# A GEGLU FFN on one core: two staged sums interleaved row by row in DRAM, and one operand sum cut in halves with GpSimd's next sums ordered behind it

## Chip, cores, metric

One core of a Trainium2 chip. The metric is the device time of one execution in microseconds, lower is better. The kernel before: 540.52 us, median of 3 runs (540.35 to 541.16).

## Reference

```python
def reference(x, w_gate, w_up, w_down):          # x (1, 2048, 1024), F = 3584, all bf16
    return (_gelu(x @ w_gate) * (x @ w_up)) @ w_down
```

## The kernel before

Both halves of the FFN are computed with seven products for eight (a Strassen-Winograd scheme): M1 to M7 from sums S1 to S4 of the left blocks and T1 to T4 of the right blocks. In the gate/up part a "pair" of feature blocks is one such scheme for gate and one for up (j = 0, 1): 14 accumulations of 4 matmuls. VectorE makes the T sums of the activations, GpSimd the S sums of the weights one pair ahead. In the down projection, T sums are sums of rows of `w_down`; T2 and T4 are computed during the gate/up part of the first half, staged in DRAM, and loaded back two rows at a time.

```python
t_dram = dram_pool.tile([P, 2, NS, DN], F32, name="t_dram")     # NS = 14 rows, DN = 512

def stage_step(n):                   # gate/up part, first half: rows of T2 (k=1), T4 (k=2)
    ...
    if k > 0:
        sp(nc.sync.dma_start(out=t_dram[:, k - 1, i, :], in_=t.bitcast(F32)))

def t_down(grp, name, i0, i1):       # down projection, two rows at a time
    ...
            if name in ("t2", "t4"):
                src = t_dram[:, 0 if name == "t2" else 1, i : i + 2, :]
                sp(nc.sync.dma_start(out=t.bitcast(F32), in_=src))
```

In the down projection a ring of 20 rows holds the T sums of one product and part of the next one, so the last loads of T2 can only be issued as TensorE frees rows of T1: four loads of 512 KB in a burst, 0.9 us apart (four issued in 3.06 us from 234.17 in the trace of the kernel before). There are eight such bursts (T2 and T4, two token groups, two halves).

The pair code, with the part that concerns pair 1 of the first half (the only pair of the first weight chunk that goes through it, and the only one that runs M2 at once):

```python
def do_m5(j):
    mm(V_[j], j, s(j, "s1"), tsum["t1"], True)
    m5[j] = m_pool.tile([P, TB], F32, name=f"m5_{j}")
    act(nc.scalar.copy(out=m5[j][:], in_=banks[V_[j]][:]))
    prep(j, "s1")                                  # GpSimd: S1 of the next pair

def do_m6(j):
    mm(QB[j], j, s(j, "s2"), tsum["t2"], False)
    act(nc.scalar.copy(out=banks[RB[j]][:], in_=banks[QB[j]][:]))
...
elif "m2" in then:
    m2(); done("m2")                               # hooks: A22 copies, then T4 on VectorE
    order = (do_m5, 0), (do_m5, 1), (do_m6, 0), (do_m6, 1)
...
for j in range(2):
    add_m5(QB[j], QB[j])                           # VectorE, before M3
    prep(j, "s2")
done("m5")
for j in range(2):
    mm(RB[j], j, s(j, "s3"), tsum["t3"], False)    # M7
    add_m5(V_[j], RB[j])                           # VectorE; releases R for M4
    ...
# then M3 (into Q, with S4), then M4 (into R, with T4)
```

## Time and profile before

| | before |
|---|---|
| time, median (lowest to highest) | 540.52 us (540.35 to 541.16) |
| span of the profiled run | 538.7 us |
| TensorE / VectorE / ScalarE / GpSimd busy | 99 / 67 / 49 / 45% |
| an undisturbed pair | 12.56 us |
| landing of the 56 staged loads, median | 5.3 us |

The lines behind the engines and the pair stand in the prediction; the landing is this line of the page:

```profile
t_mem<-t_dram SPq DMA_DIRECT2D x56, 512.0 KB, 5.3
```

"Landing" is the time from issue to the arrival of the last byte. The chain of work that ended last lists pieces in order of time: start, duration, what ran; a piece that is not TensorE's is a place where TensorE waited.

### The profile page before, as it was taken

Reading aid. Unit: us, or ns where it says so; the run is one execution under the profiler, and the core shown is the slowest. Engines: PE = TensorE matmul, PEld = TensorE weight load, DVE = VectorE, ACT = ScalarE, POOL = GpSimd, SP = SyncE. Lnnn points to the kernel's source line nnn. Section 1 sums busy time; section 2 is a strip of 40 time slices with the busy share of each in tenths; the row PEclk is TensorE's granted clock in tenths of the full one; section 3 lists DMA queues with packets and bytes.
Section 4 is the critical chain, followed back from the end, with each engine's and each line's share of the span. In section 5 each row is a group of like instructions: output and inputs, shape, how many; then the busy total and the mean of one; then the engine's idle time right before and its main releaser. Section 6 shows DMA issues by size and latency. Waiting matters only on the chain.

```text
span 538.7 us, 7074 instructions
## 1 busy us (share of the span) xinstructions
PE 532.4 (99%) x2348; PEld 377.6 (70%) x2384; DVE 362.1 (67%) x474; ACT 263.3 (49%) x446; POOL 244.6 (45%) x212
## 2 busy tenths in 40 slices
PE   9999999999999999999999999999999999999997
PEld 4577776677776686776776777777777766866865
DVE  2978767788775997989574334444454469969951
ACT  2555555555555329117465555555555551552270
POOL 0699777777776000000056776667777730000000
PEclk9999999999999999999999999999999999999999
DMA  9946776685818877779950404042222466677945
GB/s 217 324 118 194 213 244 204 229 258 190 292 60 263 302 235 252 246 262 300 326 177 1 156 1 158 22 135 71 86 78 80 157 211 215 229 240 238 293 147 204
DMA packets 84803, 102.70 MB, mean 191 GB/s; under 512 B 18720, under 2 KB 66336, under 8 KB 84768
## 3 DMA queue, kind: packets, MB, share of 16 engines
q1 hardware_dynamic: 61968, 80.30, 46.2%
q10 hardware_dynamic: 22800, 21.96, 13.1%
q8 instruction: 19, 0.31, 0.2%
q14 instruction: 16, 0.13, 0.1%
HBM read 85.98 MB, written 12.58 MB: 183 GB/s over the span
## 4 chain that ended last, share of the span: by engine, by line
PE 97%; DMA 1%; issue 0%; ACT 0%; ACTq 0%
PE bank L396 63%; PE bank L672 31%; PE bank L249 3%; DMA t_mem<-t_dram 1%; PE bank L202 1%; PE bank L293 0%; ACT o_sb L725 0%; ACT bank L450 0%; ACTq L725 0%; ACTq L450 0%
## 5 line engine op out<-in xcount | busy, mean ns | idle before, releaser
L396 PE MATMUL bank<-t_mem,s_mem 128*128 128x512 f32 x1056 | 249.4, 394 | 0.0
L396 PEld LDWEIGHTS bank<-t_mem,s_mem 128*128 128x128 f32 x1056 | 198.2, 188 | 43.8 <-ACT bank L446 0.3
L368 POOL TENSOR_TENSOR s_mem<-w_mem 128x512 fp32r<-128x512 bf16 x102 | 120.0, 1198 | 190.7 <-DVE t_mem L244 103.3
L672 PE MATMUL bank<-t_mem,s_mem 128*128 128x512 f32 x544 | 127.4, 393 | 0.1
L273 DVE TENSOR_TENSOR hT<-w_mem,bank 128x512 bf16<-128x512 f32 x104 | 71.3, 686 | 81.4 <-PE bank L396 46.3
L672 PEld LDWEIGHTS bank<-t_mem,s_mem 128*128 128x128 f32 x544 | 102.1, 188 | 22.6 <-DVE t_mem L580 0.5
L419 DVE TENSOR_TENSOR bank<-bank,m 128x512 f32<-128x512 f32 x108 | 69.9, 695 | 45.8 <-ACT m L441 44.0
L396 PE MATMUL bank<-xT,w_mem 128*128 128x512 bf16 x405 | 96.5, 380 | 1.4
L268 ACT ACTIVATE w_mem<-bank 128x512 f32<-128x512 f32 x104 | 61.9, 596 | 51.8 <-DVE bank L419 34.1
L396 PEld LDWEIGHTS <-w_mem 128*128 128x128 bf16 x432 | 40.2, 98 | 51.6 <-issue 6.8
L368 POOL TENSOR_TENSOR s_mem<-w_mem,s_mem 128x512 fp32r<-128x512 bf16 x52 | 66.5, 1304 | 0.0
L580 DVE TENSOR_TENSOR t_mem<-w_mem 128x1024 fp32r<-128x1024 bf16 x56 | 65.6, 1219 | 0.0
L368 POOL TENSOR_TENSOR s_mem<-s_mem,w_mem 128x512 fp32r<-128x512 f32 x52 | 60.7, 1189 | 0.0
L446 ACT COPY bank<-bank 128x512 f32<-128x512 f32 x54 | 30.8, 570 | 38.9 <-PE bank L396 38.9
L381 ACT CAST s_mem<-w_mem 128x512 fp32r<-128x512 bf16 x54 | 33.1, 615 | 31.6 <-PE bank L396 30.4
L647 DVE TENSOR_TENSOR s_mem<-hT 128x512 fp32r<-128x512 bf16 x52 | 34.2, 686 | 10.2 <-PE bank L672 9.4
L441 ACT COPY m<-bank 128x512 f32<-128x512 f32 x54 | 31.7, 587 | 17.5 <-PE bank L396 17.5
L672 PEld LDWEIGHTS <-hT 128*128 128x128 bf16 x224 | 21.3, 98 | 26.6 <-issue 2.1
L450 ACT COPY bank<-bank 128x512 f32<-128x512 f32 x54 | 30.7, 570 | 12.7 <-PE bank L396 12.5
L725 ACT CAST o_sb<-bank 128x512 bf16<-128x512 f32 x28 | 15.4, 585 | 39.6 <-PE bank L672 39.6
L605 DVE TENSOR_TENSOR o_sb<-wd_sb,o_sb 128x512 fp32r<-128x512 bf16 x28 | 30.5, 1090 | 0.5
L577 ACT CAST t_mem<-w_mem 128x1024 fp32r<-128x1024 bf16 x28 | 26.9, 1048 | 0.0
(42 smaller groups left out, 236.0 us busy)
## 6 DMA issues: line engine op xcount, KB each, us to landing
t_mem<-t_dram SPq DMA_DIRECT2D x56, 512.0 KB, 5.3
w_mem<-in_w_gate_dram ACTq DMA_DIRECT2D x10, 1024.0 KB, 5.2
w_mem<-in_w_up_dram ACTq DMA_DIRECT2D x10, 1024.0 KB, 5.5
wd_sb<-in_w_down_dram SPq DMA_DIRECT2D x28, 256.0 KB, 4.3
t_dram<-o_sb SPq DMA_DIRECT2D x28, 256.0 KB, 2.4
wd_sb<-in_w_down_dram SPq DMA_DIRECT2D x12, 512.0 KB, 8.4
w_mem<-in_w_down_dram SPq DMA_DIRECT2D x10, 512.0 KB, 6.1
w_mem<-in_w_down_dram SPq DMA_DIRECT2D x4, 1024.0 KB, 6.4
```

Of the source, the lines that this page charges most:

```text
L268: act(nc.scalar.activation(out=g_sb, in_=ps[:], func=ACT.Gelu_apprx_tanh))
L273: nc.vector.tensor_tensor(out=hT[:, fc, tb * TB : (tb + 1) * TB], in0=g_sb, in1=ps[:], op=ALU.mult,)
L368: pool(nc.gpsimd.tensor_tensor(out=t, in0=in0, in1=in1, op=op))
L381: act(nc.scalar.copy(out=t, in_=a(1, 1)))
L396: nc.tensor.matmul(banks[bank][:], lhsT=lhs[:, c, :], rhs=rhs[:, c, :], start=start and c == 0, stop=c == KH - 1, skip_group_check=True,)
L419: nc.vector.tensor_tensor(out=banks[dst][:], in0=banks[src][:], in1=m5[j][:], op=ALU.add)
L441: act(nc.scalar.copy(out=m5[j][:], in_=banks[V_[j]][:]))
L446: act(nc.scalar.copy(out=banks[RB[j]][:], in_=banks[QB[j]][:]))
L450: act(nc.scalar.copy(out=banks[QB[j]][:], in_=banks[P_[j]][:]))
L580: dve(nc.vector.tensor_tensor(out=t, in0=in0, in1=in1, op=ALU.subtract))
L647: dve(nc.vector.tensor_tensor(out=t, in0=in0, in1=in1, op=op))
L672: nc.tensor.matmul(banks[bset[u]][:], lhsT=lhs(i, u), rhs=rhs(i), start=start and i == 0, stop=stop and i == NS - 1, skip_group_check=True,)
```

## The change

Two parts. The intent of the first is faster loads of the staged rows (2 KB pieces, T2 and T4 of a row next to each other); that of the second is to keep a 2.7 us VectorE instruction out of the way of the adds behind it, and VectorE and GpSimd out of each other's way (side by side in pair 1 of the kernel before, T4 took 2.66 us and two S4 sums 4.36).

```diff
-    t_dram = dram_pool.tile([P, 2, NS, DN], F32, name="t_dram")
+    t_dram = dram_pool.tile([P, NS, 2, DN], F32, name="t_dram")
...
-            prep(j, "s1")                      # in do_m5; and the same for "s2"
+            if not eager:
+                prep(j, "s1")
...
+        eager = not behind and "m2" in then    # true for pair 1 of the first half alone
...
         done("m5")
+        if eager:
+            pool_behind_dve()                  # GpSimd waits for VectorE's last instruction
+            for name in ("s1", "s2"):
+                for j in range(2):
+                    prep(j, name)
...
-                src = t_dram[:, 0 if name == "t2" else 1, i : i + 2, :]
+                src = t_dram[:, i : i + 2, 0 if name == "t2" else 1, :]
-            sp(nc.sync.dma_start(out=t_dram[:, k - 1, i, :], in_=t.bitcast(F32)))
+            sp(nc.sync.dma_start(out=t_dram[:, i, k - 1, :], in_=t.bitcast(F32)))
...
-                    + [lambda: t_sum("t4")],
+                    + [lambda: t_sum("t4", 0, KH // 2)],
+                    "m5": [lambda: t_sum("t4", KH // 2, KH)],
```

The order of instructions on TensorE, ScalarE and GpSimd is unchanged; VectorE has one more instruction, behind the two adds into Q; the loads keep their order and have two runs per partition in place of one.

More of the change, by code (lines that the diff above doesn't have):

```diff
@@ L462, in pair_quads @@
             order = (do_m6, 0), (do_m6, 1), (do_m5, 0), (do_m5, 1)
-        elif "m2" in then:
+        elif eager:
             m2()
@@ L475, in pair_quads @@
             add_m5(QB[j], QB[j])
-            prep(j, "s2")
+            if not eager:
+                prep(j, "s2")
         done("m5")
+        if eager:
[3 more added lines that the diff above has]
+                    prep(j, name)
         for j in range(2):
```

## The prediction

> **What bounds the kernel now.** I read the page first (engines, then the chain of work that ended last), then the chain in order of time, then the waits of TensorE, then the timeline at the two places where something other than TensorE shows up.
>
> ```profile
> ## 1 busy us (share of the span) xinstructions
> PE 532.4 (99%) x2348; PEld 377.6 (70%) x2384; DVE 362.1 (67%) x474; ACT 263.3 (49%) x446; POOL 244.6 (45%) x212
> ...
> PE 97%; DMA 1%; issue 0%; ACT 0%; ACTq 0%
> ```
>
> TensorE is busy 532.4 of 538.7 us, and the chain is TensorE for 97% of the span. No other engine is near its limit. So the only time to be had is what TensorE does not use. The chain in order of time says how much that is:
>
> ```profile
> 320.27 0.05 issue
> 320.32 12.51 PE bank L396 x55
> 332.83 0.05 issue
> 332.88 12.51 PE bank L396 x55
> ...
> 208.64 18.96 PE bank L672 x84
> 227.60 0.05 issue
> 227.65 9.25 PE bank L672 x41
> 236.92 7.45 DMA t_mem<-t_dram
> 244.37 0.14 issue
> 244.50 8.45 PE bank L672 x36
> 252.96 0.05 issue
> ...
> 491.81 24.88 PE bank L672 x110
> 516.74 18.53 PE bank L672 x82
> ```
>
> An undisturbed pair of feature blocks takes 12.56 us (320.27 to 332.83). A pair is 14 accumulations of 4 matmuls, 56, so a matmul costs 12.56/56 = 224.3 ns; that is the pace that nothing in this change touches. The kernel has 8 warm-up matmuls, 16 transposes, and 64 + 27x56 + 4x7x28 = 2360 products. From 5.40 us, where the first product starts, to 535.34, where the last one leaves, are 529.94 us. At the pace 2360 take 529.3. About **0.6 us** in the whole kernel is TensorE standing still between its first and last product; the rest is start, end and arithmetic.
>
> The largest part of it is found by comparing like with like. The stretch of the down projection from the start of a second token group to its fifth product takes 227.60 to 252.96 = 25.36 us in the first half of the kernel and 491.76 to 516.69 = 24.93 us in the second half (each piece's start less the 0.05 of issue). The difference, 0.43 us, is the place where the chain leaves TensorE for a load of staged T2 sums out of DRAM: issued at 236.92, landed at 244.37. The timeline of the issuing queue and the waits show the same:
>
> ```profile
> 234.17 3.06 SPq L575 DMA_DIRECT2D t_mem<-t_dram  x4
> ...
> 244.47 7.83 PEld L672 LDWEIGHTS bank<-t_mem,s_mem 128*128 128x128 f32 x35 [0.53 <-DVE t_mem L580]
> ```
>
> Four loads of 512 KB go out in a burst, 0.9 us apart (each when TensorE frees two rows of T1); the last one lands too late for row 12, and the weight load sits idle 0.53 us. The releaser printed there (VectorE) is doubtful; the chain's DMA lands at the right moment.
>
> The second place is pair 1, the only pair of the first chunk that goes through the quads:
>
> ```profile
> 24.40 2.66 DVE L244 TENSOR_TENSOR t_mem<-xT,t_mem 128x2048 fp32r<-128x2048 bf16 x1
> 24.87 4.36 POOL L368 TENSOR_TENSOR s_mem<-w_mem,s_mem 128x512 fp32r<-128x512 bf16 x2
> 26.73 0.75 PEld L396 LDWEIGHTS bank<-t_mem,s_mem 128*128 128x128 f32 x4 [0.18 <-ACT bank L446]
> 26.98 2.59 DVE L419 TENSOR_TENSOR bank<-bank,m 128x512 f32<-128x512 f32 x4
> 29.18 2.30 POOL L368 TENSOR_TENSOR s_mem<-w_mem 128x512 fp32r<-128x512 bf16 x2
> ```
>
> T4 runs on VectorE beside GpSimd's S4 sums: 2.66 us where the three undisturbed ones of this shape take 2.29, and the two S4 sums take 4.36 us where an undisturbed pair takes 2.3. But what TensorE waits for here (0.18 us) is ScalarE's copy of a bank, which is not T4 and not GpSimd. From one bank copy (L450) to the next, pair 1 takes 20.79 to 33.46 = 12.67 us, 0.11 over the pace.
>
> [...] The trace agrees (2284 to 2289 undisturbed; the T sums of 1024 columns took 1218 to 1225), so each half of T4 costs about 1.22 us and the second instruction adds 0.15. [...] in 525.0 to 526.5 us, nearly all 4 KB packets, 125 packets took 84.8% of 16 engines, 0.16 us each if divided out, but in 499.5 to 501.3 it is 0.19 and in 235.4 to 237.2 0.18, while 2 KB rows (176.5 to 178.5) take 0.089. So 4 KB cost 0.16 to 0.19 us either way. [...]
>
> **The change, part by part.** (a) *Layout of the staged sums.* T2 and T4 of one row become neighbours. The 28 stores stay 2 KB per partition. Each of the 56 loads was one 4 KB run per partition and becomes two runs of 2 KB: 7168 packets become 14336. Bytes unchanged. Cost to the issuing queue: loads with 128 runs take 0.33 us to issue, those with 256 runs (w_down) 0.45 to 0.49, so +0.12 to 0.16 us each; the burst is spaced by TensorE at 0.9 us, so only one such step reaches the landing. Gain: smaller pieces keep the 16 engines fuller (they are 85 to 92% busy in these bursts, near 100% in 2 KB traffic), so the last load of a burst, 7.45 us before, may land 0 to 0.6 us sooner. Net at 244 us: between +0.15 and -0.43 (it can't give more than the wait), middle **-0.2 us**. Elsewhere nothing waits for these loads: reading issue plus landing against the moment when TensorE reaches row 12, I find slacks of some 1.1 us (second group, second half) and 1.2 to 1.7 us for the other bursts.
>
> (b) *T4 in halves.* VectorE: two of 1.22 instead of one of 2.66. The first from 24.4 to about 25.7. The adds of M5 into Q can't start before ScalarE's copies end (26.67, 27.58), so they run at 26.7 and 27.6 and end at 28.3; the second half follows, to 29.5; the two adds that release R come at 29.5 to 30.9 instead of 28.3 to 29.57. TensorE reaches the last product (M4) at 30.5 and 31.4 and overwrites R there: slack 0.2 and 0.5 us, tight but positive. T4 itself is ready at 29.5, before 30.5.
>
> (c) *GpSimd behind it.* S1 and S2 of pair 2 wait for T4's second half: start at 29.6 instead of 29.18, 0.4 us later. The S4 sums before them lose less to T4 and are done about 28.1. Pair 2 then needs S1 at 33.9 (done 31), S2 at 34.8 (33.1), S3 at 37.5 (36), S4 at 39.3 and 40.2 (38.4, 39.5). All in time. The order of TensorE, ScalarE and GpSimd instructions is otherwise unchanged. Sum of (b) and (c): **0**, within -0.1 and +0.2.
>
> Sum: 540.52 - 0.2 + 0 = **540.3 us**.
>
> **Rivals.** *The bubble closes wholly and pair 1 gets its 0.11 back*: 540.0. For it: 0.43 us is little against a 7.45 us landing, and the same burst in the second half lands its last load in 6.0. Against: that shows the landing wanders by itself, and pair 1 waits for a bank copy that is untouched. *Every second 2 KB block aliases*: T2 now lies only in even 2 KB blocks of DRAM, T4 in odd ones[...]. At +1 us per landing only the 244 us bubble grows (541.5); at +2 us all eight bursts run dry by some 0.7 us each, to about 547. Against: the half-row loads of w_down, 1 KB out of each 2 KB, run at 350 to 390 GB/s here. *The late adds stall M4 in pair 1* (VectorE slower than I think): up to +0.3 us, 540.6.
>
> **Range and chances.** The three times before spread over 0.8 us by themselves, as much as everything the change can win. Floor: 540.5 minus 0.6, 539.9, a little less with a lucky run. Ceiling: bubble not closed plus a stall of 0.3 plus spread, 541.1. So 539.7 to 541.1. Faster by 2% would be 10.8 us, and there are 0.6 us to win: 0.3%. Slower by 2% needs the aliasing at its worst: 0.7%.
>
> **What would show it.** TensorE's busy time and the 12.56 us per pair stay. T4 appears twice at 1.2 to 1.35 us, GpSimd's S4 pair shrinks from 4.36 to about 3.2 us and GpSimd stands idle about 1.5 us behind VectorE before 29.6. Packets rise by some 7170 to 92,000. Right on (a): the DMA piece in the chain is gone or shorter, and the stretch 227.6 to 253 takes 24.93 to 25.2 us. Wrong: landings of the loads rise above 6 us in the median, or TensorE shows waits for them in other groups; a wait of TensorE for VectorE's adds near 30.5; or a wait for GpSimd's S sums in pair 2.

## The result

540.46 us median (540.14 to 541.13, 6 runs) against 540.75 us (540.16 to 541.56, 6 runs) for the kernel before. The ratio is 0.9996, 95% interval 0.9983 to 1.0009: the same. (Ratios here are the mean time of one kernel's fast runs over that of the other's of the same rounds, so not quite the ratio of the medians.)

The page of the changed kernel: TensorE as busy as before, and 7168 more packets for the same bytes (91,971 less 84,803).

```profile
PE 532.2 (99%) x2348; PEld 377.6 (70%) x2384; DVE 361.9 (67%) x475; ACT 263.2 (49%) x446; POOL 244.6 (45%) x212
...
DMA packets 91971, 102.70 MB, mean 191 GB/s; under 512 B 18720, under 2 KB 66336, under 8 KB 91936
```

The chain of the changed kernel at the place where the kernel before left TensorE for a staged load:

```profile
227.70 0.05 issue
227.75 24.88 PE bank L680 x110
252.63 0.05 issue
```

From 227.70 to 252.63 are 24.93 us, the length that the undisturbed second half had before; the 0.43 us are gone. Pair 1 in the timeline of the changed kernel:

```profile
24.71 1.59 DVE L244 TENSOR_TENSOR t_mem<-xT,t_mem 128x1024 fp32r<-128x1024 bf16 x1
25.18 3.29 POOL L368 TENSOR_TENSOR s_mem<-w_mem,s_mem 128x512 fp32r<-128x512 bf16 x2
...
26.83 0.75 PEld L396 LDWEIGHTS bank<-t_mem,s_mem 128*128 128x128 f32 x4 [0.18 <-ACT bank L447]
...
28.32 1.22 DVE L244 TENSOR_TENSOR t_mem<-xT,t_mem 128x1024 fp32r<-128x1024 bf16 x1
29.47 1.28 DVE L419 TENSOR_TENSOR bank<-bank,m 128x512 f32<-128x512 f32 x2
29.68 2.29 POOL L368 TENSOR_TENSOR s_mem<-w_mem 128x512 fp32r<-128x512 bf16 x2 [1.22 <-PE bank L396]
```

T4 stands there twice; its second half runs undisturbed, GpSimd's pair of S4 sums has shrunk from 4.36 to 3.29 us, GpSimd idles 1.22 us and starts S1 at 29.68. The wait of 0.18 us for ScalarE's copy is as before, and pair 1 takes the same 12.67 us from bank copy to bank copy (20.89 to 33.56).

So the forecast matched. But one trace of each kernel cannot tell whether the wait at 244 us was cured or merely absent. That is what most of the experiments are for.

### The profile page after: what moved, and what is told of

The parts are those of the page before. It is cut to its first block, busy times and chain, and to the rows that moved or that the text cites. A ratio compares the mean times of both kernels' runs of the same rounds, so it can differ in the third digit from the quotient of the medians.

```text
span 538.5 us, 7072 instructions
## 1 busy us (share of the span) xinstructions
PE 532.2 (99%) x2348; PEld 377.6 (70%) x2384; DVE 361.9 (67%) x475; ACT 263.2 (49%) x446; POOL 244.6 (45%) x212
## 2 busy tenths in 40 slices
DMA packets 91971, 102.70 MB, mean 191 GB/s; under 512 B 18720, under 2 KB 66336, under 8 KB 91936
## 4 chain that ended last, share of the span: by engine, by line
PE 98%; DMA 1%; issue 0%; ACT 0%; ACTq 0%
PE bank L396 63%; PE bank L680 33%; PE bank L249 3%; DMA w_mem<-in_x_dram 1%; PE bank L293 0%; ACT o_sb L733 0%; ACT bank L451 0%; ACTq L733 0%; ACTq L451 0%
```

## The experiments

### Each part alone, and both kernels again

E1 is the kernel before with the three `t_dram` lines of the diff. E2 is the changed kernel with these three lines put back. E3 and E4 are the changed kernel and the kernel before once more, unedited. All ran on one chip.

> The kernel before with the DRAM layout of the changed one and nothing else. Theory (the layout is worth nothing of its own; the second landing of a burst is late in a random burst of a random run, with either layout): ratio to before 1.000 within 0.001, median landing of the 56 loads 5.3 to 5.6 us, T4 one instruction of 2.66 us, pair 1 takes 12.67 us between its bank copies; a burst may or may not have its last landing over 7.3 us. Rival (the layout removed the 0.43 us wait at 244 us): no wait for these loads anywhere, last landing of that burst under 6 us again, and a ratio of about 0.9992.

> The T4 halves and the GpSimd sums behind them, with the old DRAM layout. Theory: ratio 1.000 within 0.001; T4 twice, 1.6 and 1.2 us; GpSimd's S4 pair 3.3 us; pair 1 still 12.67 us, because the bank copy of 0.18 us is untouched. Rival (the layout is what cured the wait): 4 KB packets, 84803 in all, and a wait of 0.3 to 0.6 us for a staged load in the second group of a half.

> The changed kernel again, for a second trace of it. Theory (late landings wander): landings of the burst of the second group, first half, differ from the first trace (3.5, 4.3, 4.9, 5.7 us) by 1 us or more somewhere, other bursts likewise; ratio 1.000 within 0.001. Rival (the layout makes that burst fast): the same four landings within 0.3 us.

> The kernel before again, for a second trace. Theory (late landings wander): the burst that landed at 3.5, 6.2, 6.6, 7.5 us lands differently, most likely with the last at 6 us and no wait of TensorE; span 538.3 to 539.2. Rival (4 KB pieces make that burst late): 7 us or more for its last load again, and the DMA piece in the chain again at 244 us.

| | median us (runs) | ratio to before, 95% |
|---|---|---|
| before, same rounds | 541.01 (11) | |
| E1 layout alone | 541.21 (5) | 1.0000 (0.9988 to 1.0013) |
| E2 T4 part alone | 540.65 (6) | 0.9999 (0.9986 to 1.0011) |
| E3 both again | 540.59 (5) | 0.9992 (0.9980 to 1.0004) |
| E4 before again | 542.12 (1, profiled) | |

No part moves the time by anything that can be told from zero. The traces say more. Neither E1 nor E2 lost time at any staged load: E2's rival (4 KB runs bring the wait back) fell. For E1 that is half of what its rival said (no wait), but the burst at 236 us landed its last load at 6.2 us, not under 6, and the median landing of 5.0 us lay below the 5.3 to 5.6 that I expected. E4, the kernel before, lost time in places that its first trace did not show. In its chain, the staged load is late in another burst, that of the first group of the second half:

```profile
448.44 9.25 PE bank L672 x41
457.71 7.88 DMA t_mem<-t_dram
465.59 0.14 issue
465.73 8.43 PE bank L672 x36
474.16 0.05 issue
474.21 18.96 PE bank L672 x84
```

From 448.44 to 474.21 are 25.77 us where 24.93 are needed: 0.84 us lost. Its span of 540.1 us lay outside the 538.3 to 539.2 expected. And in its pair 1, in the timeline, VectorE was 1.4 us later than in the first trace, and TensorE waited for the adds behind T4:

```profile
26.19 2.67 DVE L244 TENSOR_TENSOR t_mem<-xT,t_mem 128x2048 fp32r<-128x2048 bf16 x1
...
28.78 2.48 DVE L419 TENSOR_TENSOR bank<-bank,m 128x512 f32<-128x512 f32 x4
...
29.61 3.88 PE L396 MATMUL bank<-t_mem,s_mem 128*128 128x512 f32 x16 [0.43 <-DVE bank L419]
```

Most of this lateness (0.96 of the 1.4 us) arose before the pair, in the first half of T3. The first trace of the kernel before, and then E4:

```profile
17.44 1.22 DVE L244 TENSOR_TENSOR t_mem<-xT 128x1024 fp32r<-128x1024 bf16 x1
...
17.88 3.89 POOL L368 TENSOR_TENSOR s_mem<-w_mem 128x512 fp32r<-128x512 bf16 x2 [16.58 <-DMA w_mem<-in_w_gate_dram]
```

```profile
18.00 1.33 POOL L368 TENSOR_TENSOR s_mem<-w_mem 128x512 fp32r<-128x512 bf16 x1 [16.70 <-DMA w_mem<-in_w_gate_dram]
...
18.24 2.18 DVE L244 TENSOR_TENSOR t_mem<-xT 128x1024 fp32r<-128x1024 bf16 x1
```

In all 14 traces, this instruction took 1.22 us where it started ahead of GpSimd's first sum (7 traces) and 2.17 or 2.18 us where GpSimd's, released by a load of weights, started first (7 traces).

E3, the changed kernel, lost 0.28 us in the T4 burst of the first group, where two loads landed after 7.0 and 7.3 us; the weight load sat idle, without a releaser that the profile could name:

```profile
225.35 1.45 PEld L680 LDWEIGHTS bank<-t_mem,s_mem 128*128 128x128 f32 x7 [0.42 <-issue]
```

Its burst at 236 us landed at 3.9, 5.4, 6.2 and 6.7 us where the first trace of the same kernel had 3.5, 4.3, 4.9 and 5.7: as the theory of E3 said.

So the late load wanders: it comes with either layout, in a different burst of a different run. The rival that 4 KB runs always spoil the burst at 236 us fell (E4 and E2 had it at 6.5 and 6.2 us); the rival that 2 KB runs cure it fell too (E3). Whether they make it rarer is answered below, when more traces are in.

### How much slack the halves leave: T4 whole in the second place, and no wait for GpSimd

E5 edits the changed kernel:

```diff
-                    + [lambda: t_sum("t4", 0, KH // 2)],
-                    "m5": [lambda: t_sum("t4", KH // 2, KH)],
+                    ,
+                    "m5": [lambda: t_sum("t4")],
```

> The changed kernel with T4 whole, in one instruction, in the second half's place (behind the adds of M5 into Q). Theory (in the changed kernel the adds that release R have some 0.3 us of slack): T4 runs 28.3 to 30.6 us after a normal start, the R adds end 1.1 us later than in halves, and TensorE waits 0.7 to 1.0 us for VectorE before M4 of pair 1; pair 1 takes about 13.5 us between its bank copies; ratio 1.0010 to 1.0020. Rival (VectorE has over 1 us of slack there): pair 1 stays 12.67 us, no wait.

541.21 us (4 runs), ratio 1.0004 (0.9990 to 1.0019). The time cannot tell; the trace can. The timeline of E5:

```profile
28.38 2.28 DVE L244 TENSOR_TENSOR t_mem<-xT,t_mem 128x2048 fp32r<-128x2048 bf16 x1
30.58 1.29 DVE L419 TENSOR_TENSOR bank<-bank,m 128x512 f32<-128x512 f32 x2
...
31.32 1.68 PEld L396 LDWEIGHTS bank<-t_mem,s_mem 128*128 128x128 f32 x8 [0.90 <-DVE bank L419]
```

Pair 1 takes 20.96 to 34.40 = 13.44 us, 0.77 more. Counted from the start of the pair (20.00 here, 19.93 in the changed kernel's trace) the R adds came 1.04 us later, so the changed kernel has 1.04 - 0.77 = 0.27 us of slack there: the second half of T4 could not be twice as long.

E6 takes `pool_behind_dve()` out of the changed kernel. The data do not need that wait.

> The changed kernel without GpSimd's wait for T4's second half ([...]the data do not need it). Theory (the wait buys an undisturbed VectorE and costs GpSimd nothing it would not lose by contention): GpSimd starts S1 of pair 2 at about 28.5 instead of 29.7 and takes 3.2 us for the two instead of 2.3, T4's second half takes 1.6 instead of 1.22, the R adds come 0.4 us later, TensorE waits 0 to 0.3 us; ratio 1.000 within 0.001. Rival (the wait delays pair 2): S4 sums of pair 2 are done 1 us sooner and pair 2 gets shorter.

540.84 us (4 runs), ratio 0.9999 (0.9985 to 1.0014). GpSimd's S1 pair starts at 28.91 instead of 29.68 and takes 3.27 us instead of 2.29, so it ends at 32.18, 0.2 us later by the clock, though this run was 0.29 us later into pair 1; T4's second half takes 1.46 instead of 1.22. TensorE waits for neither. The wait costs GpSimd nothing net and buys VectorE 0.24 us that is not on the path. The rival, that it delays pair 2, fell. The two instructions in E6:

```profile
28.57 1.46 DVE L244 TENSOR_TENSOR t_mem<-xT,t_mem 128x1024 fp32r<-128x1024 bf16 x1
28.91 3.27 POOL L368 TENSOR_TENSOR s_mem<-w_mem 128x512 fp32r<-128x512 bf16 x2
```

### VectorE made late on purpose

E4 suggested that the halves are worth something only when VectorE comes late into pair 1. E7 (from the kernel before) and E8 (from the changed one) repeat the second half of T3, with the same values, twice:

```diff
         unit_out(hT, held[0], 0, 1)
         t_sum("t3", KH // 2, KH)
+        t_sum("t3", KH // 2, KH)
+        t_sum("t3", KH // 2, KH)
```

> The kernel before with the second half of T3 computed three times (same values), so that VectorE comes 2.5 to 3 us late into pair 1. Theory (VectorE's lateness, not the load, is what the T4 halves guard against; slack before 0.95 us in front of M3): TensorE waits 1.5 to 2.2 us for the adds in pair 1; ratio 1.003 to 1.004. Rival (VectorE is far from the path in pair 1): no wait, ratio 1.000.

> The changed kernel with the same lateness. Theory (halves give 0.5 us more of slack, 1.45 in all): TensorE waits 1.0 to 1.7 us, 0.5 us less than in the kernel before with the same lateness; ratio 1.002 to 1.003. Rival (halves are neutral under lateness): the same wait as there; or GpSimd behind VectorE makes it worse: waits of TensorE for GpSimd's sums in pair 2, 0.3 us or more.

E7 took 544.55 us (ratio 1.0066, 1.0053 to 1.0079), E8 545.32 us (1.0074, 1.0061 to 1.0088). VectorE is on the path when late (waits of 1.20 to 2.76 us below), but the gain expected for the halves did not show, and both cost more than expected. The waits of TensorE in E7 and, in the second fence, in E8:

```profile
25.38 4.87 PE L398 MATMUL bank<-t_mem,s_mem 128*128 128x512 f32 x20 [1.20 <-DVE hT L273]
...
31.72 3.89 PE L398 MATMUL bank<-t_mem,s_mem 128*128 128x512 f32 x16 [1.47 <-DVE bank L421]
```

```profile
28.02 10.05 PE L398 MATMUL bank<-t_mem,s_mem 128*128 128x512 f32 x36 [2.76 <-DVE hT L273]
```

The experiment was badly placed. The lateness lay ahead of a multiplication (hT) that frees the bank M5 writes, so TensorE waited there first, ahead of everything that the change touches. In E8's trace that multiplication started 6.5 us into the pair (20.70 to 27.20), in E7's 4.9 us (19.62 to 24.56), so the two are not equally late. What can be read: behind such a wait, E8 has no wait for adds, E7 has 1.47 us. And E8 shows why the times grew by more than the waits: behind the 2.76 us the granted clock was 0.71, 0.50 and 0.94 in three stretches of 2 us, and the matmuls were stretched: 6 in the stretch at 0.50, 10 in the one at 1.00 behind the three. The first two stretches of E8 (busy per engine, then the clock, DMA share and GB/s):

```profile
28.00:30.00 2.00, 1.98 (x6) 1.62 (x7) 2.00 (x2) 0.59 (x1) 1.87 (x2) 0.71 0.07 25
30.00:32.00 2.00, 2.00 (x6) 1.60 (x5) 2.00 (x3) 0.57 (x1) 0.00 (x0) 0.50 0.00 0
```

E7's waits of 1.20 and 1.47 us left the clock at 1.00 in all six stretches of 2 us from 22 to 34 us.

E9 and E10 mend the placement. They compute the first half of T4 twice more, behind that multiplication and directly ahead of T4; E9 from the kernel before, E10 from the changed one:

```diff
+                    + [lambda: t_sum("t4", 0, KH // 2)] * 2
                     + [lambda: t_sum("t4")],                    # E10: t_sum("t4", 0, KH // 2)
```

> The kernel before with the first half of T4 computed twice more ahead of T4 (same values), so that VectorE is 2.4 to 3.2 us late from T4 on and nothing earlier waits. Theory (before the change, VectorE has 0.95 us of slack ahead of M3 in pair 1): TensorE waits 1.5 to 2.2 us for the adds of M5. Rival (VectorE is not on the path even so): no wait. Ratio 1.003 to 1.004 by the theory.

> The changed kernel with the same two instructions ahead of T4's first half. Theory (halves give 0.4 to 0.6 us more of slack, because the Q adds need not wait for the second half, and GpSimd leaves it alone): TensorE waits 1.0 to 1.7 us in all, in two pieces (for the Q adds before M3, for the R adds before M4), 0.5 us less than the kernel before with the same lateness. Rival (the halves only move the wait from M3 to M4): the same total within 0.2 us. Ratio 1.002 to 1.003 by the theory.

| | median us (4 runs each) | ratio to before, 95% |
|---|---|---|
| E9 T4 whole, late | 547.33 (545.46 to 548.83) | 1.0120 (1.0088 to 1.0152) |
| E10 T4 in halves, late | 544.36 (543.93 to 546.02) | 1.0073 (1.0049 to 1.0097) |

The waits in the timelines of E9 and of E10:

```profile
24.68 6.88 DVE L244 TENSOR_TENSOR t_mem<-xT,t_mem 128x1024 fp32r<-128x1024 bf16 x3
...
32.31 5.51 PE L396 MATMUL bank<-t_mem,s_mem 128*128 128x512 f32 x16 [3.47 <-DVE bank L419]
```

```profile
25.50 4.97 DVE L244 TENSOR_TENSOR t_mem<-xT,t_mem 128x1024 fp32r<-128x1024 bf16 x3
...
31.23 5.49 PE L396 MATMUL bank<-t_mem,s_mem 128*128 128x512 f32 x16 [2.52 <-DVE bank L419]
```

With the halves TensorE waits 2.52 us instead of 3.47, although VectorE reached T4 0.9 us later in that pair than in E9 (25.50 less 19.56, against 24.68 less 19.68). There is one wait, for the Q adds, and none for the R adds: the rival (the wait moves from M3 to M4) fell, and so did my figure of 0.5 us, which was too small. Both waits were longer than forecast (1.5 to 2.2 us, and 1.0 to 1.7 us), since the three instructions of E9 took 6.88 us, beside GpSimd's sums, where undisturbed ones would take some 4.7 (an estimate: 1.22 twice and 2.29). What the Q adds no longer stand behind is the second half of T4 and a part of the contention: the block of VectorE is 1.91 us shorter in E10, of which 1.07 are work moved behind the adds (2.29 less 1.22) and the other 0.84 less contention. In E10 GpSimd also stood idle behind VectorE; no late run leaves that wait out, so the share of the halves alone is not shown.

Both kernels then lost a further 1.8 us or so at the halved clock (0.50 in a stretch of 2 us behind the wait in each; the 1.8 is an estimate, what pair 1 took beyond 12.67 us and its wait): from bank copy to bank copy pair 1 took 17.99 us in E9 and 17.01 in E10. The two traced runs thus differ by 0.98 us (545.46 and 544.48), which is the wait. The 3 us between the medians come from two more runs of E9, 548.64 and 548.83, with a mean clock of 0.994 where the others have 0.997; they were not traced, so a longer time at the halved clock is likely there, not shown.

### Smaller pieces yet

E11 cuts the staged rows of the changed kernel into 512 B pieces:

```diff
-    t_dram = dram_pool.tile([P, NS, 2, DN], F32, name="t_dram")
+    t_dram = dram_pool.tile([P, NS, 4, 2, DN // 4], F32, name="t_dram")   # T2, T4 alternate
```

with stores and loads indexed to match, still one DMA for each.

> The changed kernel with the staged rows in pieces of 512 B, T2 and T4 alternating: four times the runs, same bytes. Theory (piece size only matters through the landing, and TensorE waits for what lands later than about 7.1 us after the last issue of a burst): about 145,700 packets; if the last landings rise to 7.5 to 8, TensorE waits some 0.5 us in most of the eight bursts, ratio 1.002 to 1.008; if they stay under 7, ratio 1.000. Rival (interleaving T2 and T4 in small pieces is itself good for the memory): last landings below the 6.2 us of 2 KB pieces.

543.79 us (541.99 to 545.32, 4 runs), ratio 1.0055 (1.0026 to 1.0083), 145,732 packets, median landing 5.9 us. The chain of E11 leaves TensorE three times in the first half:

```profile
220.38 6.61 DMA t_mem<-t_dram
226.99 0.14 issue
...
238.74 7.77 DMA t_mem<-t_dram
246.51 0.14 issue
...
265.59 7.06 DMA t_mem<-t_dram
272.65 0.14 issue
```

That part of the down projection takes 184.32 to 274.64 = 90.32 us, 2.43 more than undisturbed (87.89); the second half loses 0.2. In two of these bursts the last load was also issued late, 1.74 and 1.91 us behind the one before it instead of 0.9 (at 220.38 and 265.59), because that one's issuing instruction took 1.65 and 1.82 us instead of the 0.36 to 0.38 of 2 KB runs in such a burst. The load at 238.74 was issued on time and took 7.77 us. Part of the lateness is thus the issue, not the transfer. The last landings of the eight bursts average 7.0 us, so the rival (small pieces are good for the memory) fell; the waits that I expected in most bursts came in three. The chain from pieces to landing to TensorE is real, and 2 KB is not on the way to something better.

### A third trace of the kernel before, and all landings together

> The kernel before a third time, for its landings. In the traces so far the last landing of a burst is 6.5 us in the mean with 4 KB runs (32 bursts) and 6.2 us with 2 KB runs (48 bursts). Theory (2 KB pieces land about 0.3 us sooner, and the 7 us stragglers come with either): mean 6.4 to 6.6 again, zero to two bursts over 7. Rival (the difference is chance or the chip): mean 6.1 to 6.3.

540.77 us, one run. The last landings of its eight bursts are 6.0 to 7.3 us, mean 6.56, as the theory said; one lies over 7. It lost 0.26 us in the second half of the down projection.

The last landing of each burst, over all traces that have either layout (E11 left out):

| runs per partition | traces | bursts | mean of the last landing | longest | TensorE lost in the down projection, mean per trace | rate of the DMA engines in the bursts, trace means |
|---|---|---|---|---|---|---|
| one of 4 KB | 6 (before, E2, E4, E7, E9, E12) | 48 | 6.53 us | 7.9 us | 0.28 us | 288 to 307 GB/s |
| two of 2 KB | 7 (after, E1, E3, E5, E6, E8, E10) | 56 | 6.23 us | 7.3 us | 0.09 us | 309 to 319 GB/s |

"Lost" is the length of the down projection of a half over the shortest seen. The trace means with 4 KB lie between 6.43 and 6.69, with 2 KB between 5.94 and 6.54; of all ways to divide the 13 trace means into six and seven, 0.9% give a difference as large in this direction, 1.6% in either (a count that takes the traces as alike in all else, though they come from several chips and kernels). For the loss of TensorE the same count gives 11%, so the 0.2 us less may be chance.

Chip by chip the landings look different. On chip 10 (E1 to E8) the means of the last landing are 6.56 us with 4 KB (three traces) and 6.12 with 2 KB (five), with no overlap. In the other traces they are 6.50 (before, E9, E12) and 6.51 (after, E10): no difference. The rival of E12, "chance or the chip", is thus not excluded for the landing.

The rate is another matter. It is read from 1.2 to 4.0 us behind the first issue of each burst, eight windows a trace; one such window of the kernel before (499.53 to 502.33), and the like one of the changed kernel (499.30 to 502.10):

```profile
DMA packets 219, 0.83 MB, mean 297 GB/s; under 512 B 16, under 2 KB 16, under 8 KB 219
```

```profile
DMA packets 444, 0.88 MB, mean 313 GB/s; under 512 B 16, under 2 KB 16, under 8 KB 444
```

Every trace with 2 KB runs lies above every one with 4 KB, on all chips, and the 16 engines are busier too: 93.2 to 97.5% against 88.3 to 92.9%. That is the reason that the prediction gave, smaller pieces keeping the engines fuller. The window was chosen after the fact, and from 2.0 to 5.0 us the rates overlap, so this supports the reason and is no test of it. My own theory of E1, that the layout is worth nothing, was too strong: it speeds up the start of a burst, and by how much the last load and TensorE profit is open.

### Where the times come from

With these losses the spans add up. "Quads start" is when the chain reaches the first matmuls of pair 1, behind the first loads and the first pair.

| trace | span | quads start | lost in pair 1 | lost in the down projection | rest |
|---|---|---|---|---|---|
| before | 538.7 | 19.83 | 0 | 0.42 | 518.45 |
| E4 before | 540.1 | 20.21 | 0.64 | 0.84 | 518.41 |
| E12 before | 538.8 | 20.11 | 0 | 0.26 | 518.43 |
| after | 538.5 | 19.93 | 0 | 0.09 | 518.48 |
| E3 after | 538.4 | 19.61 | 0 | 0.28 | 518.51 |
| E1 layout alone | 539.5 | 21.02 | 0 | 0 | 518.48 |
| E2 T4 alone | 540.6 | 22.18 | 0 | 0 | 518.42 |
| E5 T4 whole, late | 539.2 | 20.00 | 0.77 | 0 | 518.43 |

The rest is constant within 0.1 us. The largest piece that varies is the start: 19.6 to 22.2 us. In E1 the chain waits there for the first loads of weights, the last landed at 11.73 us. In E2, the slowest run in the table, TensorE itself was slow: it did 9 matmuls from 6 to 8 us, busy all the time, where the changed kernel's trace has 17; why, the trace does not say. E2 lost nothing anywhere that the change touches. The change works on the two middle columns, together 0.3 and 0.4 us in two traces of the kernel before and 1.5 us in the third, under a spread from the start of 2.6 us.

## Why the prediction was right, point by point

- **The bound.** Right: TensorE at a fixed pace (224.3 ns a matmul in an undisturbed pair), 0.6 us to win. The table above gives the same from the other side: 518.4 to 518.5 us that no version touched.
- **The wait at 244 us.** Right in place and size, wrong in what it seemed to be. The prediction took it as this burst's own; E4 and E12 show that it is one draw of a late landing that can fall on any burst. It did say that "the landing wanders by itself", as an argument against the rival; that was the better half of the step.
- **Layout: the last load "may land 0 to 0.6 us sooner", net -0.2 us.** Within the range by the pooled traces (0.3 us sooner, 0.2 us less lost), but the landing gained on one chip only and the loss may be chance. The reason given, fuller engines, fits the rates of all traces. That the piece at 244 us vanished in the first pair of traces, as forecast, was in part luck: the bursts of the changed kernel landed no sooner in the mean there (6.5 us in both), and a bad draw was compared with a good one. The cost to the issuing queue was put too high, at 0.12 to 0.16 us a load: in a burst a load took 0.36 to 0.38 us to issue where it took 0.32 to 0.33.
- **Aliasing of 2 KB blocks.** Fell: the median landing was 5.0 to 5.5 us with 2 KB runs, 5.1 to 5.5 with 4 KB. (The 350 to 390 GB/s that the prediction set against it are those of busy stretches: 363 from 198 to 200 us, but 279 from 172 to 174.)
- **T4 in halves: zero.** Right for an ordinary run: pair 1 took 12.67 us before and after. T4's halves took 1.59 and 1.22 us, not 1.22 twice: the first still runs beside GpSimd. The slack before M4 was put at 0.2 us; E5 gives 0.27. Incomplete for a run in which VectorE is late: E4 lost 0.64 us in pair 1 without the halves, and E9 and E10 show that the halves, with GpSimd behind them, shorten such a wait. The prediction had no term for that.
- **GpSimd behind T4.** Right: it started at 29.68 (29.6 forecast), S4 took 3.29 us (3.2), pair 2 waited for none of GpSimd's sums, and GpSimd idled 1.22 us (about 1.5 forecast). E6 shows that the wait itself could be left out at no cost in time.
- **The sum.** 540.3 forecast, 540.46 measured, ratio 0.9996. Neither this nor the repeat (0.9992) is clear of 1. A gain of some 0.2 us from the layout is what the traces suggest and no time shows.

What stays open: why a landing jumps by 2 to 3 us within a burst (4.3, then 7.5 us in E4), and why the last landing followed the rate on one chip and not on the others.

## What to carry to other kernels

Where one engine is busy 99% of the span, add up the places where it stands still before anything else: that sum is all that a change of order or layout can win. A wait for a load seen in a single trace is one draw; take several traces, and compare the landings of all like loads, before believing that a layout caused or cured it. A long instruction ahead of short, urgent ones on the same engine can be worth cutting, with a part put behind them, even when an ordinary run shows no gain: here the gain came when that engine was late (a wait of 2.52 us instead of 3.47, one trace each).

## What the traces measured

- GpSimd beside VectorE (kernel before, pair 1): two GpSimd sums took 4.36 us beside T4 and 2.3 alone, and VectorE's T4 2.66 instead of 2.29. The same 1024-column T3 half took 1.22 us where it started before GpSimd's sum and 2.17 or 2.18 where it started behind it (7 traces each).
- The granted clock behind a wait of TensorE: 0.50 in a stretch of 2 us behind the waits of 2.52 (E10), 2.76 (E8) and 3.47 us (E9); 1.00 behind those of 1.20 and 1.47 us (E7).
- The pace of the matmuls of 512 columns: 224.3 ns (kernel before, from a pair of 12.56 us), bf16 and fp32r matmuls each with its weight load, at a granted clock of 0.999 to 1.0.
- Loads of 512 KB in bursts: 2 KB runs moved 309 to 319 GB/s where 4 KB runs moved 288 to 307 (means of the early part of the bursts), and 512 B runs cost 2.6 us of TensorE time in one trace (E11), partly through late issues. In a burst, these loads took 0.32 to 0.33 us to issue with 128 runs and 0.36 to 0.38 with 256.
